# Folding the channels a second time per slot, with pooled queries as 128 and 16

## The chip, the cores and the metric

The kernel runs on one NeuronCore of a Trainium2 chip. Its engines are TensorE (PE, with its weight loads shown as PEld), VectorE (DVE), ScalarE (ACT), GpSimd (POOL) and SyncE (SP, which here only issues DMAs). The metric is the device time of one launch in microseconds, the median of several runs.

## The reference

Inputs q, k and v have the shape (8 batches, 8 heads, 576 positions, 64 channels); w_ch1 is 512 x 2048 and w_ch2 is 2048 x 512. All is float32.

```python
# attention: pooled by 4, and local within a band of |i - j| < 4
q_d, k_d, v_d = (x.reshape(B, H, 144, 4, D).mean(axis=3) for x in (q, k, v))
out_up = np.repeat(softmax_attention(q_d, k_d, v_d), 4, axis=2)
out_local = softmax_attention_masked(q, k, v, mask=abs(i - j) < 4)
x = heads_side_by_side(out_up + out_local)          # (8, 576, 512)
# mixing: the real part of a Fourier transform over positions and channels
mixed = np.real(np.fft.fft(np.fft.fft(x, axis=1), axis=2))
u = x + mixed
# feed-forward on the normalised rows
un = (u - mean(u)) / sqrt(var(u) + 1e-6)
out = u + relu(un @ w_ch1) @ w_ch2
```

## The kernel before

The work has two stages that overlap. In the first, for each of the 8 batches, attention and the Fourier mixing run; their results go to two tensors in HBM, `ud` (the pooled result, each row repeated four times) and `um` (the local result plus the mixed one). In the second, the feed-forward network (FFN) takes nine blocks of 512 rows, in four tiles of 128 each. A block's tile is loaded from `um` by SP and then `ud` is added to it by an accumulating DMA that POOL issues (`Block.load`, L695 to 707). Then come statistics and normalisation (L709 to 726), transposition on PE (L728), splitting into a high and a low part (L737 to 745), and the two products of the network (L754 to 781).

Matrix products here use a float32 type that PE takes rounded, so each operand is split: a high part by a rounding copy on ACT, and a low part by a subtraction, on POOL or DVE. A product is then three: high by high, high by low, low by high.

**Attention.** `Unit` (L352) is one of five local units per batch; each computes two windows of 64 positions for all 8 heads. `Pooled` (L240) works on two heads at a time: scores, maxima (DVE), exponentials (ACT), transposition of the probabilities (PE), a copy (ACT), the product with the values and the division (DVE). It has 144 queries in two halves of 72 (`GH`), and the results lie in `odt`, 72 partitions by 2 halves by 512 channels. The local results lie in `xa` (positions from the start) and `xb` (from the end), three slots of 128 partitions each; of the third slot only rows 0 to 63 are used and the rest is cleared once (L221).

**Mixing.** `Mix` (L506) uses symmetry. `half_sum` (DVE, L514) and `half_difference` (POOL, L518) fold the positions: x(s) + x(-s) and x(s) - x(-s). Then `channels_even` and `channels_odd` (DVE, L528 to 535) fold the channels: c with 512 - c, 256 channels each, for three local slots and for the two halves of `odt`. `split_high` (ACT) and `split_low` (POOL) make the operands `fh` and `fl`. `sequence` (PE, L564) transforms the positions: for each of 4 groups T of 128 channels, 3 x 5 products of 320 columns against the cosine and sine tables `seqm` and `seqg`. `sequence_z` (L580) does the same for the middle channel, which the folding leaves over. After another splitting, `mix` (PE, L593) transforms the channels: for each of three slots, an even and an odd part of 512 columns, 6 products each, and one more for the middle channel. `mixed` (DVE, L609) adds that to the local result, `unfold` (POOL, L615) undoes the folding of positions, and `store` (SP, L623) writes `um`.

**The order of the work** is written out by hand. Each piece is put on a timetable by `at(t, fn)`; all pieces are sorted by t and issued in that order, and each engine then runs its own queue strictly in order. `PACE` is 20, so batch b's pieces lie near t = 20 b; a step of the timetable is no fixed time. The numbers are in the table `AT` (L22 to 52). For batch b, `mix_at(b)` is 20 b plus the entry `mix`; from there, `halves` gives the first half sum, its step per slot, the first half difference and its step; `splits` the same for folds and splits; `z` and `sequence` the sequence products; `mixed` the first mix product, the step between the six of them, and the delays of `mixed`, `unfold` and `store`. The pooled part has its own start `pooled_at(b)` and end `pooled_end(b)`.

**Memory** is reused in four steps. At `t_b` the pooled part's tiles are given up (`close_b`, L830) and the four tiles of block 0 (`uts[0]`) take their place. At `t_a` the local part's are given up (`close_a`, L835), and there the tiles of block 1, the transposed operands `unT0`, more buffers for the weights and four PSUM banks for the FFN's results come in. `t_e` and `t_d` (L846, L852) follow when the tables of sequence and of channels are no longer needed. The weights arrive in an 8-byte form and are rebuilt by ACT, POOL and DVE in quarters of a tile pair (`Quarter`, L135); the first three tile pairs during attention, the next ones from `t_a` on.

**The passage from attention to FFN** goes so: block 0 is loaded from `t_b` on (L862), normalised from `t_a` on (L864), and its first five tile pairs of weights (`ROUND`) run, then five of block 1, while the last batch is still mixed.

## Time and profile before

| what | value |
|---|---|
| median of 3 runs | 1250.82 us (1249.33 to 1250.82) |
| the profiled execution, its time | 1254.06 us |
| its span, first to last instruction | 1252.0 us |
| mean granted PE clock | 0.967 of full speed |
| PE, PEld busy | 1184.1, 981.2 us |
| DVE, ACT, POOL busy | 590.7, 356.0, 318.2 us |
| read from and written to HBM | 81.82 MB, 28.34 MB |

A page of the profile gives the busy time of each engine as a union of its instructions' intervals, the span in 40 slices with the busy share in tenths, the chain of work that ended last, and groups of instructions by line. In a group's row, the line and the engine come first, then the operation, what it writes and reads, its shapes and count, then the busy time and the mean length of one, then the engine's idle time just before and who ended it. PE's matrix products are pipelined: the length of one is longer than the distance from one to the next, and what a series costs is read from the chain's pieces or the timeline. A row of a table of stretches gives each engine's busy time in that stretch, the granted clock, the share of the DMA engines and what they moved.

### The profile page before, as it was taken

How to read it: one execution, taken by the hardware profiler on the slowest of the kernel's cores; microseconds unless marked ns; L12 is line 12 of the kernel's file. 1: busy time of each engine (PE TensorE's matmuls, PEld its weight loads, DVE VectorE, ACT ScalarE, POOL GpSimd, SP SyncE). 2: the span in 40 equal slices, each digit the busy share in tenths (PEclk: the TensorE clock that was granted, in tenths of full speed). 3: DMA queues.
4: the chain of work that ended last, by engine and by line, in shares of the span. 5: the costliest groups of instructions: out<-in, count | busy, mean ns of one | idle time of the engine just before them, and what ended most of it. 6: DMA issues, size and time to landing. Idle time of an engine off the chain costs nothing.

```text
span 1252.0 us, 20525 instructions
## 1 busy us (share of the span) xinstructions
PE 1184.1 (95%) x8336; PEld 981.2 (78%) x8336; DVE 590.7 (47%) x1218; ACT 356.0 (28%) x1038; POOL 318.2 (25%) x397
## 2 busy tenths in 40 slices
PE   5889998899995699999999999999999999999998
PEld 5777887787984578888888888888888888888887
DVE  3767778698877788853222222122122222221211
ACT  3655454555562333431111111111011111111100
POOL 2226355365456566531010010000100100100000
PEclk7888998999997799999999999999999999999999
DMA  9755484565645525314040120210400400300000
GB/s 293 197 169 134 128 238 110 162 196 172 163 127 153 133 77 155 119 51 101 5 97 1 52 50 1 78 25 1 99 3 1 101 1 1 101 1 1 34 1 34
DMA packets 50462, 111.45 MB, mean 89 GB/s; under 512 B 6120, under 2 KB 6248, under 8 KB 50040
## 3 DMA queue, kind: packets, MB, share of 16 engines
q1 hardware_dynamic: 42000, 88.66, 22.6%
q0 software_dynamic: 8368, 21.48, 9.3%
q8 instruction: 66, 1.08, 0.4%
q14 instruction: 28, 0.23, 0.1%
HBM read 81.82 MB, written 28.34 MB: 88 GB/s over the span
## 4 chain that ended last, share of the span: by engine, by line
PE 81%; DVE 10%; DMA 6%; POOL 1%; SPq 1%; issue 1%; ACT 1%; POOLq 0%
PE hps L761 31%; PE acc L779 10%; PE acc L781 10%; PE acc L780 10%; PE y L569 4%; PE mix L607 4%; DMA vsum<-in_vg_dram 3%; PE av L452 2%; DMA qkT<-in_qk_dram 2%; PE avd L307 2%; PE sc L393 1%; DVE sums L379 1%; DVE xeo L535 1%; PE tpn L732 1%; PE sp L262 1%
## 5 line engine op out<-in xcount | busy, mean ns | idle before, releaser
L761 PE MATMUL hps<-unT,w1h 128*128 128x512 f32 x1152 | 311.5, 392 | 0.6 <-DVE yl L578 0.6
L769 DVE SCALAR_TENSOR_TENSOR hl<-hps,hh 128x512 fp32r<-128x512 f32 x144 | 99.3, 690 | 437.3 <-ACT hh L765 437.3
L761 PEld LDWEIGHTS hps<-unT,w1h 128*128 128x128 f32 x1152 | 215.2, 188 | 46.7 <-DVE yl L578 0.8
L765 ACT ACTIVATE hh<-hps 128x512 fp32r<-128x512 f32 x144 | 86.2, 598 | 512.1 <-PE hps L761 512.0
L779 PE MATMUL acc<-w2h,hh 128*128 128x512 f32 x576 | 226.5, 393 | 0.0
L781 PE MATMUL acc<-w2h,hl 128*128 128x512 f32 x576 | 225.1, 391 | 0.0
L780 PE MATMUL acc<-w2l,hh 128*128 128x512 f32 x576 | 225.0, 391 | 0.0
L761 PE MATMUL hps<-unT,w1l 128*128 128x512 f32 x576 | 155.2, 391 | 0.0
L761 PEld LDWEIGHTS hps<-unT,w1l 128*128 128x128 f32 x576 | 108.1, 188 | 23.8
L781 PEld LDWEIGHTS acc<-w2h,hl 128*128 128x128 f32 x576 | 108.2, 188 | 23.6
L779 PEld LDWEIGHTS acc<-w2h,hh 128*128 128x128 f32 x576 | 108.1, 188 | 22.9
L780 PEld LDWEIGHTS acc<-w2l,hh 128*128 128x128 f32 x576 | 108.2, 188 | 22.8
L717 POOL TENSOR_TENSOR rstd<-rstd,mhalf 128x1 f32<-128x1 f32 x36 | 20.3, 564 | 341.4 <-DVE rstd L716 341.4
L704 POOL DMA_DIRECT2D ut<-ud x40 | 35.5, 1111 | 208.0 <-DMA ut<-um 207.7
L607 PE MATMUL mix<-chanm,yh 128*128 128x512 f32 (+1 forms) x192 | 65.8, 425 | 5.6 <-DVE xs L611 3.7
L411 ACT ACTIVATE sb<-sc,mx 128x64 f32<-128x64 f32 x320 | 69.8, 329 | 1.3
L741 DVE TENSOR_TENSOR unT<-tpn,unT 128x512 fp32r<-128x512 f32 x36 | 24.8, 690 | 90.4 <-ACT unT L738 90.4
L547 POOL TENSOR_TENSOR fl<-xeo,fh 128x512 fp32r<-128x512 f32 (+1 forms) x40 | 56.0, 1404 | 30.5 <-ACT fh L542 30.2
L379 DVE TENSOR_REDUCE sums<-qkT 128x224 f32<-128x896 f32 (+4 forms) x48 | 44.5, 947 | 27.9 <-DMA qkT<-in_qk_dram 19.6
L520 POOL TENSOR_TENSOR xm<-xa,xb 128x512 f32<-128x512 f32 x24 | 34.2, 1427 | 87.9 <-DVE xb L470 79.9
L738 ACT CAST unT<-tpn 128x512 fp32r<-128x512 f32 x36 | 21.0, 586 | 113.5 <-PE tpn L732 113.5
L452 PE MATMUL av<-vaug,pT 64*64 64x65 f32 x1280 | 48.5, 227 | 1.7 <-DVE odt L322 1.5
(102 smaller groups left out, 1579.7 us busy)
## 6 DMA issues: line engine op xcount, KB each, us to landing
qkT<-in_qk_dram SPq DMA_DIRECT2D x40, 512.0 KB
raw<-in_wq_dram SPq DMA_DIRECT2D x64, 256.0 KB
vaug<-in_vw_dram SPq DMA_DIRECT2D x40, 260.0 KB
ud<-odt SPq DMA_DIRECT2D x16, 576.0 KB
out_dram<-ut SPq DMA_DIRECT2D x36, 256.0 KB
ut<-um SPq DMA_DIRECT2D x32, 256.0 KB
ut<-ud POOLq DMA_DIRECT2D x32, 256.0 KB, 5.6
vsum<-in_vg_dram POOLq DMA_DIRECT2D x24, 292.5 KB, 4.5
```

What stands on the lines that cost most here:

```text
L379: nc.vector.tensor_reduce(out=to, in_=x[:, :, a - g0 : e - g0], axis=AX.X, op=ALU.add)
L411: nc.scalar.activation(out=self.sb[:, a], in_=self.sc[:, a * W : (a + 1) * W], func=AF.Exp, scale=0.125, bias=self.mx[:, a : a + 1],)
L452: nc.tensor.matmul(av[r, a, :], pT[r, 4 * hh + a], va[r, 4 * hh + a, :], start=True, stop=True)
L547: nc.gpsimd.tensor_sub(out=l, in0=self.x[t], in1=h.bitcast(F32))
L569: nc.tensor.matmul(y, l, r, start=(i == 0), stop=(i == len(mms) - 1))
L607: nc.tensor.matmul(to, l, r, start=(i == 0), stop=(i == len(mms) - 1))
L761: nc.tensor.matmul(hps, a[:, c, :], unT[:, x, c, :], start=(i == 0), stop=(i == len(mms) - 1))
L765: nc.scalar.activation(out=hh, in_=self.hps[f], func=AF.Relu)
L769: nc.vector.scalar_tensor_tensor(out=hl, in0=self.hps[f], scalar=0.0, in1=self.hh[f].bitcast(F32), op0=ALU.max, op1=ALU.subtract)
L779: nc.tensor.matmul(acc, hh, w2h, start=start, stop=False)
L780: nc.tensor.matmul(acc, hh, w2l, start=False, stop=False)
L781: nc.tensor.matmul(acc, hl, w2h, start=False, stop=stop)
```

## The change

- **Channels folded a second time.** After the first fold, c with 512 - c (`channels`, on DVE, now both signs by one function and 255 channels wide), a second one folds c with 256 - c (`fold`): the sums on DVE, the differences on POOL, 2 x 128 channels each. Channels 0 and 256 go apart, with four columns in `z` in place of two. The groups T are now: sums and differences of the even fold, sums and differences of the odd fold. Even output channels need only two of the groups and odd ones the other two, so the channel table `chanm` has 256 columns in place of 512, and `mix` makes two half-width series where there was one of full width. `mixed` reads the two halves interleaved.
- **Pooled queries as 128 and 16.** In place of two halves of 72, the first 128 queries are one operand, and the last 16 go into rows 64 to 79 of the third local slot of `xa`, which were free. So the sequence products have four operands per series in place of five, and the table `seqg` is gone: its rows lie in `seqm`, which has a fourth slot. Maxima are four reductions per pair of heads in place of two, and the division has two multiplications in place of one. Storing the pooled result takes four DMAs in place of three.
- **Block 0's tokens loaded early.** `uts[0]` is a tile of its own from the start; its loads are on the timetable at 120, 124, 128 and 132, the accumulating ones 2.47 later. Block 0's normalisation is tied to `t_b` in place of `t_a`, and its operands lie in the memory given up at `t_b`.
- **Order set anew.** Nearly all entries of `AT` change.

```diff
-    "mix": (18.44, 18, 18),
+    "mix": (25.1, 24, 22.86, 21.7, 21.69),
-    "halves": (0.26, 3.82, 0.35, 3.58),
-    "splits": (1.11, 4, 0.49, 1.7, 2.25),
-    "z": (0.86, 9.92, 12.49, 12.91, 14.07),
-    "sequence": (13.12, 1.11, 2.15, 3.28),
-    "mixed": (19.5, 1.61, 1.13, 2.66, 2.85),
+    "halves": (0.3, 1.85, 0.35, 1.8),
+    "splits": (0.5, 1.8, 0.3, 0.6, 0.87, 1.4, 2),
+    "z": (0.14, 4.65, 7.44, 7.9, 8.9),
+    "sequence": (8.39, 1.11, 2.07, 3.07),
+    "mixed": (14.09, 1.4, 1.03, 2.53, 7.14),
-    "ffn": (7.51, 1.51),
+    "ffn": (4.81, 1.52),
-    "add": (2.5, 2.04, 2.98),
+    "add": (2.47, 0.77, 3.17),
...
+    queries = [(P, slice(0, P)), (G - P, slice(P, G))]
...
         def maxima(self, h0):
+            for t, (n, _) in enumerate(queries):
+                for hl, sp in enumerate(self.sps[h0]):
+                    i = 2 * t + hl
+                    nc.vector.tensor_reduce(
+                        out=mx[:n, i : i + 1], in_=sp[:n, t, :], axis=AX.X, op=ALU.max, negate=True
+                    )
...
         def result(self, h0):
+            for t, r in enumerate(rows):
+                to = (xa[r, NSL - 1] if t else odt)[:, h0 * D : (h0 + 2) * D]
+                nc.vector.tensor_mul(
...
+        def channels(self, t, odd):
+            if self.w.get(t) is None:
+                self.w[t] = psq.tile([P, 2, HD], F32, name="w", bufs=2)
+            src = odt if t == NSL else halves[self.b % 2][odd][:, t]
+            nc.vector.tensor_tensor(
+                out=self.w[t][:, odd, 1:HD],
+                in0=src[:, 1:HD],
+                in1=src[:, DM - 1 : HD : -1],
+                op=ALU.subtract if odd else ALU.add,
+            )
+        def fold(self, t, minus):
+            eng, op = (nc.gpsimd, ALU.subtract) if minus else (nc.vector, ALU.add)
+            w = self.w[t]
+            eng.tensor_tensor(
+                out=self.x[t][:, 2 * minus : 2 * minus + 2, :],
+                in0=w[:, :, 1 : P + 1],
+                in1=w[:, :, HD - 1 : P - 1 : -1],
+                op=op,
+            )
...
         def slots(self, x, odd, i):
-            groups = [(x[:GH, NSL + t], seqg[:, i, odd, t, :]) for t in range(2)]
-            return groups + [(x[:, t], seqm[:, i, odd, t, :]) for t in reversed(range(NSL))]
+            return [(x[:, t], seqm[:, i, odd, t, :]) for t in (NSL, NSL - 1, *range(NSL - 1))]
...
         def mix(self, t, odd):
+            for half, T in enumerate((3, 1) if odd else (0, 2)):
+                to = ps[:, half * HD : (half + 1) * HD]
+                for i, (l, r) in enumerate(((lh, mh), (lh, ml), (ll, mh))):
+                    nc.tensor.matmul(
+                        to, l, r, start=(bool(odd) and i == 0), stop=(i == 2), skip_group_check=True
+                    )
...
-            at(t_b + 0.1 + 0.1 * i + AT["add"][0] * pooled, blocks[0].load, i, pooled)
+            at(120 + AT["add"][0] * pooled + 4 * i, blocks[0].load, i, pooled)
...
-            (blocks[0], t_a, AT["first_norms"]),
+            (blocks[0], t_b, AT["first_norms"]),
```

More of the change, by code (lines that the diff above doesn't have):

```diff
@@ L77 @@
     c_signs: bass.AP,
-    c_group: bass.AP,
     out: bass.AP,
@@ L129 @@
     nc.vector.memset(mhalf, -0.5)
+    uts = {0: [res.tile([P, DM], F32, name=f"ut0{i}") for i in range(TILES)]}
+    unTs = {}
     ident = res.tile([P, P], F32, name="ident")
@@ L203 @@
     pd = p1.enter_context(tc.tile_pool(name="pd", bufs=1, side="right"))
-    odt = pd.tile([GH, 2, DM + 2], F32, name="odt")
-    nc.gpsimd.memset(odt[:, :, DM:], 0.0)
+    odt = pd.tile([P, DM + 2], F32, name="odt")
+    nc.gpsimd.memset(odt[:, DM:], 0.0)
+    rsd = pd.tile([P, 2, 2], F32, name="rsd")
+    nc.gpsimd.memset(rsd, 1.0)
     pbank = ExitStack()
@@ L286, in transpose_p @@
                 for kt in range(2):
-                    for t in range(2):
+                    for t, (n, cols) in enumerate(queries):
                         nc.tensor.transpose(
-                            tp[:, kt, t * GH : (t + 1) * GH],
-                            self.sd[h0][:, 2 * hl + t, kt * GH : (kt + 1) * GH],
-                            ident[:GH, :GH],
+                            tp[:, kt, cols],
+                            self.sd[h0][:n, 2 * t + hl, kt * GH : (kt + 1) * GH],
+                            ident[:n, :n],
                         )
@@ L302, in values @@
         def values(self, h0):
-            av = self.av[h0] = bank("avd", GH)[:, : 4 * (D + 1)].rearrange("p (t h d) -> p t h d", t=2, h=2)
+            av = self.av[h0] = bank("avd")[:, : 4 * (D + 1)].rearrange("p (t h d) -> p t h d", t=2, h=2)
             for hl in range(2):
-                for t in range(2):
+                for t, (n, cols) in enumerate(queries):
                     for kt in range(2):
                         nc.tensor.matmul(
-                            av[:, t, hl, :],
-                            self.pts[h0][hl][:, kt, t * GH : (t + 1) * GH],
+                            av[W * t : W * t + n, t, hl, :],
+                            self.pts[h0][hl][:, kt, cols],
                             self.vs[:, kt, h0 + hl, :],
@@ L500, in constants @@
         nc.gpsimd.dma_start(out=signs, in_=c_signs)
-        nc.gpsimd.dma_start(out=seqg, in_=c_group)
     def clear_yz():
@@ L539, in split_high @@
             if self.fh is None:
[L540 to L542 removed]
+                self.fh, self.fl = (psq.tile([P, NSL + 1, 4, P], F32R, name=f"f{part}", bufs=1) for part in "hl")
+            nc.scalar.copy(out=self.fh[:, t], in_=self.x[t])
         def split_low(self, t):
[L545 removed]
@@ L644, in plan @@
                 at(t + first_m + step_m * i, self.half_difference, slot)
-            for begin, name, these in (
-                (pooled_end(self.b), "pooled_splits", (NSL, NSL + 1)),
-                (t, "splits", local),
-            ):
-                first, step, odd, high, low = AT[name]
+            for begin, name, these in ((pooled_end(self.b), "pooled_splits", [NSL]), (t, "splits", local)):
+                first, step, odd, minus, plus, high, low = AT[name]
                 for i, slot in enumerate(these):
                     u = begin + first + step * i
-                    at(u, self.channels_even, slot)
-                    at(u + odd, self.channels_odd, slot)
+                    at(u, self.channels, slot, 0)
+                    at(u + odd, self.channels, slot, 1)
+                    at(u + minus, self.fold, slot, 1)
+                    at(u + plus, self.fold, slot, 0)
                     at(u + high, self.split_high, slot)
@@ L831, in close_b @@
         p1.close()
-        early = pool("early")
-        uts[0] = [early.tile([P, DM], F32, name=f"ut0{i}") for i in range(TILES)]
+        pools["early"] = pool("early")
+        unTs[0] = pools["early"].tile([P, 2, NCC, TILES * P], F32R, name="unT0")
     def close_a():
```

188 lines of the change are left out of this document (82 added, 106 removed).

## The prediction

> **What bounds the kernel now.** I read the page first, then a table with one row per batch, then the chain of waits, then the waits at the place where attention gives way to the feed-forward network (FFN).
>
> ```profile
> span 1252.0 us, 20525 instructions
> PE 1184.1 (95%) x8336; PEld 981.2 (78%) x8336; DVE 590.7 (47%) x1218; ACT 356.0 (28%) x1038; POOL 318.2 (25%) x397
> ```
>
> PE is busy for 95% of the span, so work taken from PE could be worth its length. But VectorE (DVE) at 47% is an average over two stages with different limits. The table of stretches, cut where each batch's sequence-z products start (columns: stretch, length, busy time of PE, PEld, DVE, ACT, POOL with counts, granted clock, DMA share, GB/s):
>
> ```profile
> 0.00:67.60 67.60, 47.05 (x716) 41.00 (x717) 39.66 (x94) 33.69 (x122) 20.34 (x35) 0.79 0.83 247
> 67.60:116.90 49.30, 46.14 (x588) 38.74 (x589) 36.15 (x83) 25.78 (x93) 19.61 (x19) 0.94 0.50 138
> 116.90:170.40 53.50, 49.08 (x604) 41.11 (x604) 39.68 (x92) 27.43 (x99) 26.44 (x29) 0.90 0.56 157
> 170.40:220.84 50.44, 46.85 (x590) 39.19 (x589) 39.43 (x88) 26.62 (x95) 22.47 (x24) 0.93 0.59 161
> 220.84:268.60 47.76, 42.82 (x544) 35.64 (x544) 37.04 (x81) 24.83 (x91) 24.78 (x27) 0.96 0.61 171
> 268.60:316.60 48.00, 45.77 (x642) 39.19 (x637) 42.28 (x97) 28.42 (x102) 26.81 (x29) 1.00 0.64 176
> 316.60:360.00 43.40, 43.26 (x589) 36.80 (x588) 38.51 (x87) 26.00 (x94) 23.81 (x25) 1.00 0.52 149
> 438.00:470.00 32.00, 31.70 (x143) 24.74 (x142) 27.98 (x49) 11.30 (x27) 19.41 (x26) 1.00 0.26 75
> ```
>
> Six periods run from 67.6 to 360.0: 48.73 us each on average, PE busy 45.65, DVE busy 38.85. PE is the fuller engine, at 0.937 of a period, but DVE is close behind (its best share is 38.51 of 43.40, 0.887). The last row shows PE full once the FFN runs. Between the two lies a hole:
>
> ```profile
> 392.00:408.00 16.00, 0.08 (x1) 0.00 (x0) 8.77 (x21) 1.84 (x5) 11.19 (x12) 0.57 0.89 229
> 408.00:424.00 16.00, 8.28 (x41) 5.78 (x41) 9.43 (x19) 3.91 (x9) 11.57 (x16) 0.71 0.72 164
> 424.00:431.00 7.00, 6.57 (x32) 6.53 (x33) 6.66 (x17) 2.90 (x9) 2.93 (x5) 0.69 0.65 172
> ```
>
> PE idles 15.9 + 7.7 + 0.4 = 24.1 us, and what it does there at clocks of 0.71 and 0.69 loses 8.28 x 0.29 + 6.57 x 0.31 = 4.4 us more. The waits of that place (from 370 to 445 us; engine and line, whom it waited for, total, times, longest) and two pieces of the chain say why:
>
> ```profile
> PE tpn L732 <- DVE un L724: 18.6, 3, 16.3
> DVE st L713 <- DMA ut<-ud: 7.0, 1, 7.0
> PE y L569 <- DVE unT L741: 5.4, 1, 5.4
> 396.82 8.17 DMA ut<-ud
> 417.11 5.30 DMA raw<-in_wq_dram
> ```
>
> Block 0's tokens are loaded only when attention closes. DVE waits 7.0 us for them with the last batch's folding queued behind that wait, and PE waits for both. A second stop of 5.4 us comes from weights that arrive late.
>
> **What PE loses.** Three pieces of the chain at full clock, and the group of weight loads:
>
> ```profile
> 360.23 1.46 PE yz L585 x10
> 361.69 2.24 PE y L569 x15
> 379.07 3.02 PE mix L607 x13
> L569 PEld LDWEIGHTS y<-seqm,fh 128*128 128x128 f32 x192 | 33.3, 202 | 0.0
> ```
>
> A sequence product takes 2.24 / 15 = 0.149 us for 320 columns. Four pooled rows of operands per chain become one, so each of the 4 chains of a batch has 12 products, not 15: 12 x 0.149 = 1.8. The z chain has 8 instead of 10: 2 x 0.146 = 0.3. A mix product takes 3.02 / 13 = 0.232 for 512 columns; 36 of the 39 per batch shrink to 256 columns. From 0.149 and 0.232 the slope is 0.083 / 192 columns, so 256 columns come to 0.121; the bound above is 0.149, the row with more columns. I take 0.126, near the slope: 36 x 0.106 = 3.8. Together 5.9 us per batch, 47 over eight. Four products of scores, four transpositions and eight value products per pair of heads keep their number and columns (128 + 16 for 72 + 72): nothing.
>
> **What DVE gains.** Rows of the batch from 316.6 to 360.0 (group, shapes, count, busy us, mean ns of one, idle before):
>
> ```profile
> L267 DVE TENSOR_REDUCE mxd<-sp 72x2 f32<-72x288 f32 x8 | 3.2, 444 | 0.0
> L406 DVE TENSOR_REDUCE mx<-sc 128x8 f32<-128x512 f32 x5 | 3.4, 682 | 0.0
> L318 DVE TENSOR_SCALAR rsd<-avd 72x4 f32<-72x4 f32 x4 | 0.6, 150 | 0.3 <-PE avd L307 0.3
> L322 DVE TENSOR_TENSOR odt<-avd,rsd 72x256 f32<-72x256 f32 x4 | 1.7, 420 | 0.1
> L531 DVE TENSOR_TENSOR xeo<-xs 128x256 f32<-128x256 f32 x3 | 2.8, 922 | 0.0
> L531 DVE TENSOR_TENSOR xeo<-odt 72x256 f32<-72x256 f32 x2 | 1.6, 790 | 0.0
> L535 DVE TENSOR_TENSOR xeo<-xm 128x256 f32<-128x256 f32 x3 | 1.3, 418 | 0.0
> L535 DVE TENSOR_TENSOR xeo<-odt 72x256 f32<-72x256 f32 x2 | 0.9, 474 | 0.0
> ```
>
> Maxima: the two reductions differ by 238 ns over 224 elements, 1.06 ns each. Eight of 288 elements become sixteen of 144, each 0.29 us alone and, by the overlap of the row (8 x 444 ns in 3.2 us), 0.25 in a row: 4.0, so +0.8. Results: per pair of heads one more 0.15 and two multiplications of 128 elements (420 - 136 = 284 ns) for one of 420: +0.3, times four, less overlap, +1.0. Folding: ten operations in 6.6 us become twelve of the same size (eight first folds, four sums; the four differences go to POOL): 12 x 0.66 = 7.9, +1.3. If all ran at the 0.41 of the undisturbed ones, it would be 4.9, so -1.7. Sum +3.1 (from 0 to +6): DVE goes from 38.85 to 42.0 per batch while PE goes to 39.8. DVE becomes the fuller engine.
>
> Why the same operation takes 0.42 or 0.92 shows in three lines of the timeline:
>
> ```profile
> 337.51 0.68 DVE L516 TENSOR_TENSOR xs<-xa,xb 128x512 f32<-128x512 f32 x1
> 345.04 1.27 POOL L520 TENSOR_TENSOR xm<-xa,xb 128x512 f32<-128x512 f32 x1
> 345.13 1.74 DVE L516 TENSOR_TENSOR xs<-xa,xb 128x512 f32<-128x512 f32 x1
> ```
>
> The sum takes 0.68 us alone and 1.74 when POOL's difference is running: it ends 0.56 after POOL does. If every new difference on POOL holds up DVE in this way for its whole length, the change can lose; that is the slower rival below, at 1269 us. The Trainium skill (SBUF — State Buffer, SBUF: two separate sides) has it as a rule: a VectorE operation with two SBUF inputs and a GpSimd operation that reads SBUF take an exclusive lock on a shared pair of ports, and the second waits until the first has ended. By that rule, the trace agrees: 1.74 is about what is left of POOL's operation and a whole sum.
>
> **The period.** At 0.937 full, 42.0 gives 44.8 us; at DVE's own best share of 0.887 it gives 47.3. I take 45.2, nearer the first: in steps of the timetable (20 to a batch; worked out from its rows mix, halves, splits and mixed) the old one lays half sums and folds at 18.3 to 29.4 over the mixing of the batch before at 17.5 to 26.7; the new one lays mixing at 15.8 to 23.8 and folds at 22.0 to 27.8, so fewer operations of DVE and POOL should meet. That is 3.5 us times six periods, 21 us.
>
> **The last two batches.** Batch 7's sequence and mix products lie where PE is full beside FFN work, so 5.9 counts whole. Batch 6's lie just ahead of the hole, where DVE finishes last: I count half, 3.
>
> **The hole.** Loading block 0 early moves four loads on SP and four accumulating ones on POOL into the seventh batch's time:
>
> ```profile
> L704 POOL DMA_DIRECT2D ut<-ud x40 | 35.5, 1111 | 208.0 <-DMA ut<-um 207.7
> ```
>
> The issue costs POOL 4 x 1.1 us, beside 24 of 43 busy: hidden. POOL's load waits for SP's to land, and differences and low parts queue behind it; the two are 2.47 steps apart, 6.0 us at 48.73 / 20 per step, against at most the 8.17 of the chain's piece: up to 2.2 us per load, which POOL's idle time holds. Batch 6's store stood behind two of the late weight fetches in SP's order and now stands behind four, which removes most of the 5.4. What remains is the last batch's own chain:
>
> ```profile
> 396.20 1.23 DVE L516 TENSOR_TENSOR xs<-xa,xb 128x512 f32<-128x512 f32 x1
> L542 ACT CAST fh<-xeo 128x512 fp32r<-128x512 f32 x3 | 1.9, 618 | 1.9 <-DVE xeo L535 1.9
> L547 POOL TENSOR_TENSOR fl<-xeo,fh 128x512 fp32r<-128x512 f32 x3 | 3.8, 1275 | 3.0 <-ACT fh L542 3.0
> L190 POOL TENSOR_TENSOR w1l<-wt,w1h 128x256 fp32r<-128x256 f32 x2 | 1.4, 724 | 2.5 <-ACT w1h L186 2.5
> ```
>
> PE stopped at 392.1, and DVE came to the last half sum at 396.2 without the load's wait. From there: sum 1.23, two first folds 0.84, POOL's difference 0.72 (a POOL operation of 256 elements, the last row), high part 0.62, low part 1.28, and some 0.5 of hand-overs, 5.2 us: the first product at 401.4, 9.3 us of idle. Normalising block 0 falls into the same stretch on DVE; at most the 8.8 us that DVE was busy from 392 to 408, of which I take 3, because PE transposes that block meanwhile. So 12 of idle and 1.5 of slow clock against 28.5: 15 us gained, bounds 5 and 25.
>
> **Waits that come new.** A slot's high part on ACT now waits for POOL's difference too; behind it stand the exponentials of the next unit. At most 4 x 0.72 = 2.9 us per batch, on an engine that is busy 26 of 43: nothing, but it may delay the scores' banks. The 16 pooled queries lie in the local slot, so DVE's next pooled result waits until the half sum, the half difference and the store have read them: 3.8 and 4.6 steps, 9 to 11 us, nothing. One more store per batch on SP, and four short scalings more on ACT: nothing.
>
> The clock is a further cost of an idle PE:
>
> ```profile
> 114.00:120.00 6.00, 3.05 (x19) 1.55 (x20) 4.24 (x14) 3.65 (x12) 2.29 (x3) 0.81 0.72 182
> 120.00:126.00 6.00, 6.00 (x33) 5.58 (x31) 2.38 (x7) 2.34 (x10) 3.73 (x6) 0.50 0.75 184
> ```
>
> After a stretch half idle PE runs 6 us at half clock, so 3 us are lost after 3 us of waiting. In the six periods the granted clocks of 0.94, 0.90, 0.93, 0.96, 1.00 and 1.00 cost 12.7 us of PE's busy time. A PE that waits for DVE may pay this more often, but then it has time to spare; I leave it inside the 45.2 and the range.
>
> **Sum.** 21 + 3 + 5.9 + 15 = 44.9. The profiled execution took 1254.06 us (span 1252.0): 1209.2. It lies 3.2 above the median of 1250.82, so 1206. Batch 0 is left as it is: its tables shrink by 1.1 MB (4.5 us of DMA at the 247 GB/s of the first row), worth 0 to 4.
>
> **Rivals.**
> - *PE's saving counts whole.* Periods shrink by 5.9: 6 x 5.9 + 5.9 + 5.9 + 20 = 67, time 1184. For it: the period from 316.6 with PE never idle. Against: 42.0 of DVE would need a 42.8 period at 0.98.
> - *DVE eats the saving.* At 47.3 per period, 6 x 1.4 + 5.9 + 10 = 24, time 1227. For it: DVE was never above 0.887.
> - *The half-width products cost nearly as much as before.* A weight load lasts 202 ns; if that set the pace, mix saves 36 x 0.030 = 1.1 instead of 3.8. Batch 7 loses 2.7 and the periods about 1 each: 1215. Against: 0.149 for a sequence product, which has the same load and is shorter than 202.
> - *Slower: the lock.* The four POOL differences of 256 elements (0.72 us) each hold DVE for their whole length, +2.9, so DVE needs 44.9, and keeps its 9.9 us of idle per period since what it waits for stays: 54.8. That is +6.1 x 6 + 3 less 15 and 5.9, time 1269. It decides from a period of about 51.7: then six periods and batch 6 cost the 20.9 that the hole and batch 7 bring. By the skill's page on SBUF this is what the lock can do at worst; the batch from 316.6, with 0.42 beside 0.92 for one kind of fold, shows that it strikes about half the time, hence the small chance.
>
> **How the numbers follow.** Forecast 0.47, whole saving 0.22, eaten 0.16, half-width 0.06, slower 0.09. The forecast's own range is 1195 to 1218. From 1178 to 1232 takes in the first four with their bounds and leaves out the slower case and the tails. A measurement can tell about 0.2%, 2.5 us. Faster 0.88 (the first four less a tail), same 0.03, slower 0.09.
>
> **What would show it.** Mix products of 256 columns 0.12 to 0.15 apart; y chains of 12 in about 1.8 us; periods near 45 with DVE at 0.9 or more and PE below it; more DVE folds longer than 0.8 us if the lock rules; PE's idle between the last local products and the first FFN products near 12 us instead of 24, with no DVE wait for block 0's load. The prediction is wrong if periods stay at 48 or above, if PE's idle there stays over 20, or if the periods fall below 43.

## The result, and the profile after

The change makes the kernel slower: 1295.06 us (1293.29 to 1296.65, 4 runs) against 1250.07 us (1248.92 to 1250.82, 4 runs) of the kernel before on the same chip, a ratio of 1.036 (95% interval 1.0342 to 1.0378), 45 us where a gain of 45 was forecast. The page of the changed kernel:

```profile
span 1292.6 us, 20563 instructions
PE 1216.6 (94%) x8224; PEld 993.8 (77%) x8224; DVE 637.3 (49%) x1362; ACT 360.3 (28%) x1062; POOL 336.0 (26%) x421
```

PE has 112 products fewer and is busy 32.5 us longer. DVE has 46.6 us more to do, POOL 17.8. The same table as before the prediction, cut where each batch's sequence-z products start (stretch, length, busy time of PE, PEld, DVE, ACT, POOL with counts, granted clock, DMA share, GB/s):

```profile
81.47:130.21 48.74, 45.93 (x526) 37.14 (x524) 38.62 (x91) 25.02 (x90) 21.55 (x24) 0.92 0.49 134
130.21:186.08 55.87, 50.82 (x575) 41.14 (x574) 46.59 (x111) 28.71 (x105) 27.65 (x32) 0.85 0.51 144
186.08:239.86 53.78, 45.78 (x556) 37.62 (x554) 43.86 (x100) 24.42 (x89) 25.27 (x28) 0.87 0.51 139
239.86:293.52 53.66, 50.68 (x575) 40.74 (x573) 43.35 (x102) 26.82 (x97) 27.60 (x30) 0.85 0.58 162
293.52:351.06 57.54, 53.56 (x575) 43.00 (x573) 45.89 (x107) 27.36 (x98) 28.14 (x30) 0.80 0.57 160
351.06:405.03 53.97, 48.05 (x575) 38.47 (x574) 45.01 (x107) 27.22 (x98) 29.18 (x33) 0.91 0.54 135
405.03:462.58 57.55, 39.56 (x397) 32.99 (x396) 41.60 (x102) 20.85 (x68) 25.13 (x30) 0.77 0.30 90
462.58:1292.60 830.02, 820.62 (x3681) 674.68 (x3679) 282.70 (x521) 143.22 (x287) 127.06 (x183) 1.00 0.18 49
```

The account of the 40.6 us between the two spans: the first batch's mixing starts at 81.5 instead of 67.6 (+13.9); seven periods take 381.1 us instead of 344.4 (+36.7); what follows the last batch's z products takes 830.0 instead of 840.0 (-9.9). The six periods compared in the prediction average 53.9 us, not 45.2 and not the old 48.7. DVE is busy 43.9 of them, or 0.81, and PE 49.1, or 0.91, at clocks of 0.80 to 0.92: neither is full over a period. Something inside the period holds both.

One period in slices shows where (same columns, from 270 us on):

```profile
270.00:276.00 6.00, 6.00 (x69) 4.33 (x67) 5.66 (x12) 1.43 (x4) 3.94 (x7) 1.00 0.82 193
276.00:282.00 6.00, 3.88 (x74) 3.46 (x74) 5.97 (x12) 3.38 (x14) 3.91 (x5) 0.86 0.84 253
282.00:288.00 6.00, 6.00 (x31) 3.63 (x28) 5.72 (x12) 2.69 (x7) 5.24 (x5) 0.50 0.88 292
288.00:293.50 5.50, 4.64 (x68) 3.99 (x68) 4.07 (x8) 2.07 (x10) 5.42 (x5) 0.50 0.40 110
```

From 270 to 288 us DVE is nearly full (5.66 to 5.97 of 6). PE idles 2.1 us, then its clock falls to 0.50, and in 282 to 288 it gets through 31 products, after 69 and 74 (in part of other kinds) in the two slices before. The timeline of that stretch (start, length, engine, line, what is written and read; in brackets the engine's idle time before it and who ended it):

```profile
276.44 1.75 DVE L526 TENSOR_TENSOR xs<-xa,xb 128x512 f32<-128x512 f32 x1
278.22 0.42 DVE L538 TENSOR_TENSOR w<-xs 128x255 f32<-128x255 f32 x1
...
279.29 0.40 PE L397 MATMUL sc<-maskb,identb 64*64 64x512 bf16 x2 [2.12 <-DVE xs L633]
...
281.82 1.71 POOL L530 TENSOR_TENSOR xm<-xa,xb 128x512 f32<-128x512 f32 x1
282.50 1.30 DVE L538 TENSOR_TENSOR w<-xs 128x255 f32<-128x255 f32 x1
283.49 1.45 POOL L565 TENSOR_TENSOR fl<-xeo,fh 128x512 fp32r<-128x512 f32 x1
283.73 1.49 DVE L551 TENSOR_TENSOR xeo<-w 128x256 f32<-128x256 f32 x1
```

DVE's lines are half sums and folds of the local slots. In the lines left out it also has maxima and `mixed` between them, and just ahead, from 273.3 to 276.4, it rebuilds weights. PE waits 2.12 us until DVE has done a `mixed` (L633) that stands in this queue. The same fold lasts 0.42 us at 278.22, where POOL does nothing, and 1.30 at 282.50, beside POOL's half difference, ending 0.27 after it. The Trainium skill (SBUF — State Buffer, SBUF: two separate sides) says that of a VectorE operation with two SBUF inputs and a GpSimd operation that reads SBUF, the one that starts first blocks the other for its whole length; the trace agrees, with the end of the fold 0.27 us behind the end of POOL's operation.

### The profile page after: what moved, and what is told of

It is laid out like the page before. It is cut to its first block, busy times and chain, and to the rows that moved or that the text cites. A ratio compares the mean times of both kernels' runs of the same rounds, so it can differ in the third digit from the quotient of the medians.

```text
span 1292.6 us, 20563 instructions
## 1 busy us (share of the span) xinstructions
PE 1216.6 (94%) x8224; PEld 993.8 (77%) x8224; DVE 637.3 (49%) x1362; ACT 360.3 (28%) x1062; POOL 336.0 (26%) x421
## 4 chain that ended last, share of the span: by engine, by line
PE 76%; DVE 13%; POOL 4%; DMA 2%; issue 2%; ACT 2%; SPq 0%; POOLq 0%; DVEq 0%
PE hps L779 30%; PE acc L799 10%; PE acc L797 10%; PE acc L798 10%; PE y L587 4%; PE avd L312 3%; DVE w L538 2%; DMA vsum<-in_vg_dram 2%; PE tp L293 2%; PE av L463 2%; PE sc L404 1%; DVE xs L526 1%; DVE xeo L551 1%; DVE wt L173 1%; PE mix L626 1%
## 5 line engine op out<-in xcount | busy, mean ns | idle before, releaser
L779 PEld LDWEIGHTS hps<-unT,w1l 128*128 128x128 f32 x576 | 108.1, 188 | 23.8
L312 PE MATMUL avd<-vsum,ptd 72*128 72x65 f32 (+1 forms) x512 | 65.2, 268 | 2.4 <-DMA vsum<-in_vg_dram 1.5
L759 DVE TENSOR_TENSOR unT<-tpn,unT 128x512 fp32r<-128x512 f32 x36 | 24.7, 689 | 84.3 <-ACT unT L756 84.3
L293 PE MATMUL tp<-ident,sd 128*72 128x128 f32 (+1 forms) x256 | 53.9, 270 | 11.5 <-DVE xm L633 6.4
L312 PEld LDWEIGHTS avd<-vsum,ptd 72*128 72x128 f32 (+1 forms) x512 | 53.4, 156 | 12.2 <-DMA vsum<-in_vg_dram 1.7
L463 PE MATMUL av<-vaug,pT 64*64 64x65 f32 x1280 | 54.1, 243 | 8.9 <-issue 7.0
L293 PEld LDWEIGHTS tp<-ident,sd 128*72 128x72 f32 (+1 forms) x256 | 29.6, 116 | 40.2 <-issue 17.4
L463 PEld LDWEIGHTS av<-vaug,pT 64*64 64x64 f32 x1280 | 48.2, 155 | 14.5 <-issue 8.9
```

The lines of the kernel that those rows point to most:

```text
L293: nc.tensor.transpose(tp[:, kt, cols], self.sd[h0][:n, 2 * t + hl, kt * GH : (kt + 1) * GH], ident[:n, :n],)
L312: nc.tensor.matmul(av[W * t : W * t + n, t, hl, :], self.pts[h0][hl][:, kt, cols], self.vs[:, kt, h0 + hl, :], start=(kt == 0), stop=(kt = ...
L463: nc.tensor.matmul(av[r, a, :], pT[r, 4 * hh + a], va[r, 4 * hh + a, :], start=True, stop=True)
L779: nc.tensor.matmul(hps, a[:, c, :], unT[:, x, c, :], start=(i == 0), stop=(i == len(mms) - 1))
```

## The experiments

The kernel before took 1251.67 to 1254.66 us beside these runs; each ratio is to the runs beside it, and differences of medians to the changed kernel are good to some 4 us (an estimate from the spread of the kernel before, 1250.07 to 1254.66). Three theories stood at first: that it costs when PE changes between widths (M), that a load of 128 columns costs more than one of 72 (W), and that DVE's extra work sets the period (D). Later came a fourth, that the new timetable costs (O).

**Wide products first.** In transpositions and value products the loop over 128 and 16 becomes the outer one; nothing else changes.

```diff
...
-            for hl in range(2):
-                for t, (n, cols) in enumerate(queries):
+            for t, (n, cols) in enumerate(queries):
+                for hl in range(2):
```

> The changed kernel, with the products of the 128-query operand first and those of the 16-query operand behind them, in the transpositions and in the value products (same work, other order inside each step). Theory M (every change between a 128-wide and a 16-wide operand stops PE for about 0.1 us): per pair of heads 12 of the 18 changes go, transpositions fall from 1.48 to about 0.85 us and value products from 1.74 to about 1.15, 1.2 us per pair, 38 us over the kernel where PE sets the pace: time 1255 to 1270. Rival W (an operand of 128 columns takes longer to load than one of 72): both stay at 1.48 and 1.74, time 1295. Rival D (DVE, 5 us more per batch, sets the pace): the pieces shrink as in M, the time stays at 1285 to 1295.

1280.42 us, ratio 1.0232 (1.0196 to 1.0267): 14.6 us of the 45, between what M (1255 to 1270) and what D and W (1285 to 1295) had foretold. Eight transpositions and sixteen value products of a pair of heads, each with what comes behind them, in the kernel before, the changed one and this one, from their timelines:

```profile
328.87 1.19 PE L307 MATMUL avd<-vsum,ptd 72*72 72x65 f32 x16
329.87 0.54 PE L569 MATMUL y<-seqg,fh 72*128 72x320 f32 x2
...
364.51 0.69 PE L288 MATMUL tp<-ident,sd 72*72 72x72 f32 x8
365.13 1.15 PE L452 MATMUL av<-vaug,pT 64*64 64x65 f32 x32
```
```profile
306.78 1.55 PE L293 MATMUL tp<-ident,sd 128*72 128x128 f32 x8
308.26 1.15 PE L463 MATMUL av<-vaug,pT 64*64 64x65 f32 x32
...
314.55 1.81 PE L312 MATMUL avd<-vsum,ptd 72*128 72x65 f32 x16
316.28 0.48 PE L619 MATMUL mix<-signs,yz 128*128 128x512 f32 x1
```
```profile
255.74 0.88 PE L292 MATMUL tp<-ident,sd 128*72 128x128 f32 x8
256.55 0.51 PE L624 MATMUL mix<-chanm,yh 128*128 128x256 f32 x2
...
258.77 1.56 PE L310 MATMUL avd<-vsum,ptd 72*128 72x65 f32 x16
260.26 1.15 PE L461 MATMUL av<-vaug,pT 64*64 64x65 f32 x32
```

The distance from the series to its successor is what it costs: 0.62 us before, 1.48 after, 0.81 with the widths grouped. Six changes of width fewer save 0.67 us, 0.11 each (M, for the transpositions). The Trainium skill says that a change of the tiling mode drains PE (TensorEngine Tiling (Array Packing), Key Properties), without a price; a cost per change would fit that, but no run here shows whether 16 rows beside 128 are such a change. The value products fall only from 1.73 to 1.49, where sixteen with 72 columns had taken 1.00 here and 1.09 in the median of the attention stage. What stays when the widths are grouped is what W foretold; that it comes from the loads is not shown.

**Early load undone.** Block 0's tiles, loads and normalisation put back as in the kernel before.

```diff
...
-            at(120 + AT["add"][0] * pooled + 4 * i, blocks[0].load, i, pooled)
+            at(t_b + 0.1 + 0.1 * i + AT["add"][0] * pooled, blocks[0].load, i, pooled)
...
```

> The changed kernel, with block 0 loaded and normalised as before, at the end of attention. All theories: the hole returns; from the traces (last sequence-z to the end: 840 us before, 830 after) about 10 us more, 1300 to 1310. If the early load's waits on POOL and SP are what slows the periods, it is faster instead: below 1280.

1301.69 us, ratio 1.041 (1.0372 to 1.0448). The early load gains, but some 6.6 us and not the 15 forecast for the hole.

**Second folding with the new order, and with the old.** Both kernels have the second folding but two halves of 72 queries and no early load. The first keeps the new timetable, the second has the old one. With the new order:

```diff
...
-    queries = [(P, slice(0, P)), (G - P, slice(P, G))]
...
+    seqg = psq.tile([GH, 2, 2, 2, NK1], F32R, name="seqg")
...
```

> The changed kernel without the pooled queries as 128 and 16 (two halves of 72 as before) and without the early load; the second folding and the new order stay. Theory M: no changes of width, PE per batch falls below that of before (mix 4 us less), so time 1230 to 1255. Rival D, if it is the folding that loads DVE: still slow, 1270 to 1300.

With the old one (here the folds of a slot follow at 0.8 and 1.1 behind its first):

```diff
...
-    "halves": (0.3, 1.85, 0.35, 1.8),
+    "halves": (0.26, 3.82, 0.35, 3.58),
...
```

> The kernel before with the second folding alone, in the old order (two halves of 72, late load). Theory M: PE 4 us less per batch, 1225 to 1250. Rival D (folding): DVE 2 to 3 us more per batch and POOL's differences in its way, 1255 to 1280. Beside the run without the split of queries but in the new order this tells what the new order is worth.

1307.03 us, ratio 1.0443 (1.0413 to 1.0474), and 1265.55 us, 1.0119 (1.0076 to 1.0161). The folding alone loses 13 us, although PE is busy 14.0 us less (1170.1): DVE has 27 us more. The new order adds 41 us to that; part of it may be that the first kernel also packs the folds of the two pooled halves into 0.7 steps (entry `pooled_splits`), closer than either timetable has them. Both ran without the change of widths, so M, which had foretold 1230 to 1255 for the first, is not the main cause. This was the turn: the order, which the prediction had counted as a gain, is the largest loss.

**The old order in the changed kernel.** Three kernels: the whole old timetable; the same with the wide products first; and the old entries for the mixing alone. In all three the half sum of the third slot runs ahead of the last pooled results that go into its free rows, so the mixing takes older rows there; number and size of the operations are those of the changed kernel.

```diff
...
-    "mix": (25.1, 24, 22.86, 21.7, 21.69),
...
-    "halves": (0.3, 1.85, 0.35, 1.8),
-    "splits": (0.5, 1.8, 0.3, 0.6, 0.87, 1.4, 2),
...
+    "mix": (18.44, 18, 18),
...
+    "halves": (0.26, 3.82, 0.35, 3.58),
+    "splits": (1.11, 4, 0.49, 0.8, 1.1, 1.7, 2.25),
...
```

> All parts of the change (second folding, 128 and 16 queries in free rows, early load), but every entry of the timetable as before (the three folds of a slot stand at +0.8, +1.1 and later in the old spacing of 4 per slot). Theory O (the new timetable, which lays the half sums and folds of three slots 1.8 apart in one stretch and the mixing after it, costs about 40 us, as the second folding with the new and with the old order show, 1307 against 1266): 1252 to 1265 us, periods of 50 to 52 us, first yz product near 71 us rather than 81. Rival D (DVE with 44 us per batch and the contention of the folds with POOL sets the period, whatever the order): 1285 to 1300 us, periods stay at 53 to 57.

> The old timetable as in the run before it, and the 128-wide transpositions and value products of a pair issued ahead of the 16-wide ones. If the two costs add (order 40 us, changes of width 15 us): 1238 to 1250 us, at or a little below the kernel before. If the period is set by DVE once the order is gone: within 5 us of the run before it.

> The changed kernel with only the timetable of the mixing as before (mix start, half sums, folds and splits, z, sequence products, mixed), while the start of the pooled attention, its steps, the loads of q, k and v and the early load keep the new one. Theory O, with its loss in the bunched folds: 1252 to 1270 us, close to the run with the whole old timetable. If the loss sits in the shift of pooled attention and loads against one another: 1285 to 1300 us.

1272.21 us (1.011 to 1.021), 1265.37 (1.0069 to 1.0133) and 1267.2 (1.0085 to 1.0168). The third is where O put it; the first lies between O and D, and the second, 7 us below the first, fits neither of its two expectations. So the entries of the mixing carry most of it, and D alone does not: all seven periods average 49.5 to 50.0 us, for 54.4 in the changed kernel and 49.2 in the kernel before, with the same 1362 operations on DVE. The 96 folds among them take 59 to 61 us in place of 75.2. But 13 to 20 us over the kernel before remain, and these kernels do not wait for the free rows. And the reason for the new order shows. The last pooled result of a batch lands 24.9 steps after 20 b in batch 0 and 20.9 in the last ones (`pooled_at` + 15 + 9.41), while the old timetable sums the third slot, where 16 of those rows now lie, at 18.3 to 18.7. The free rows forbid that.

**The folding's differences on DVE.** The prediction's slower rival named these 32 POOL operations as what holds DVE up.

```diff
-            eng, op = (nc.gpsimd, ALU.subtract) if minus else (nc.vector, ALU.add)
+            eng, op = nc.vector, ALU.subtract if minus else ALU.add
```

> The changed kernel with the differences of the second folding on DVE in place of POOL (32 operations more on DVE, none of this kind on POOL). By the lock rival of the prediction (each difference on POOL holds DVE for its own length) DVE gets the work but loses the waits: the mean of the folding operations w and xeo falls from 0.75 to 1.0 us towards 0.5 us, DVE's busy time rises by no more than 10 us and the time is 1270 to 1297 us. Without contention: the means stay, DVE's busy time rises by some 24 us (32 by 0.75), and the time rises to 1300 to 1325 us.

1295.26 us, ratio 1.0338 (1.0297 to 1.0378), no different from the changed kernel. DVE's busy time rises by 13.0 us and POOL's falls by 27.6, and on balance neither is felt. DVE's folds become 128 and take 97.7 us, 0.76 each, after 75.2 us for 96, or 0.78: they do not get shorter. So these differences are not what stretches the folds.

**Third slot second.** An order that the free rows allow: slot 1, then slot 2, then slot 0, 1.9 steps apart, the mixing started nearly as early as before, wide products first.

```diff
...
-            local = list(reversed(range(NSL)))
+            local = [1, 2, 0]
...
```

> All parts of the change and the wide products first, with an order that is the old one except that the slot with the free rows is summed second instead of first (slot 1 at step 4, slot 2 at 5.9, slot 0 at 7.8 after the start of mixing, which is 19.5, 18.6 and 18 steps), so that the 16 pooled rows are in it in time. In the runs with the old order the half sums of this slot came ahead of the last pooled results. Theory O in its narrower form (the free rows forbid the early half sums, and it is the bunching of sums and folds behind the pooled attention that costs): the three slots lie 1.9 steps apart here too, so little is won on the changed kernel with the wide products first: 1268 to 1280 us, periods 51 to 54 us. If it was the late start of the mixing (25.1 and 21.7 steps) that cost: 1245 to 1265 us, as with the old order.

1292.99 us, ratio 1.0331 (1.0296 to 1.0366): outside both expectations, and worse than the narrow form of O allowed. It is also 12.6 us above the wide products first with the new order. The early start of the mixing brought nothing here, with the three slots as close as before; why it lost, no run shows.

**Useless products in PE's idle time.** Since PE's clock falls after its idle time in the stretch, this fills it.

```diff
+            for _ in range({4: 18, 0: 8}.get(self.m, 0) if self.u >= 4 else 0):
+                to = self.av[0].rearrange("p h d -> p (h d)")
+                nc.tensor.matmul(to, seqm[:, 0, 0, 0, :P], seqm[:, 0, 0, 0, : 4 * (D + 1)], start=True, stop=True)
```

> The changed kernel with useless products put on TensorE ahead of the value products of two of a batch's five local units (18 and 8 products of 260 columns, into a bank that the value products overwrite), where TensorE waits for DVE in the stretch of the folds: about 3 us of work more per batch. Theory C (TensorE's idle time in that stretch costs twice, because the granted clock stands at 0.50 for the 12 us behind it): the clock stays nearer 1.00, the periods fall by 1 to 5 us and the time to 1260 to 1290 us, though TensorE has more to do. If the stretch of DVE and POOL alone sets the period: 1293 to 1300 us. If TensorE's own work is the path: up to 1318 us.

1292.84 us, ratio 1.0324 (1.0283 to 1.0365), and these two slices in place of the second and third above:

```profile
276.00:282.00 6.00, 5.98 (x98) 4.94 (x98) 5.86 (x12) 3.39 (x14) 3.99 (x5) 1.00 0.93 274
282.00:288.00 6.00, 3.59 (x20) 2.60 (x20) 5.79 (x12) 2.72 (x9) 5.24 (x5) 0.83 0.57 223
```

The clock is back, PE does more, and the time does not move: the seven periods take 3.3 us less together, and the first batch starts 3.2 later. PE finishes sooner and then waits for DVE, 2.41 us ahead of the transpositions at 285.56. So the half clock is here a sign of the stall more than what costs.

**Slots spread again.** Same order as the third-slot-second kernel, 3.3 to 3.5 steps apart.

```diff
...
-    "halves": (4, 1.9, 4.1, 1.8),
-    "splits": (4.2, 1.9, 0.3, 0.6, 0.87, 1.4, 1.9),
+    "halves": (4, 3.3, 4.1, 3.3),
+    "splits": (4.3, 3.5, 0.49, 0.8, 1.1, 1.7, 2.2),
...
```

> All parts of the change, wide products first, and the three slots' half sums and folds spread again (slot 1 at step 4, slot 2 at 7.3, slot 0 at 10.6 after the start of mixing at 18.44 and 18 steps; spacing 3.3 to 3.5 where the change has 1.8 and the kernel before about 4), with the slot of the free rows in second place, so that the pooled rows are in it in time; the products follow 0.7 steps later than in the old timetable. Theory O (bunching: DVE full, folds stretched by POOL's subtractions beside them, TensorE waiting): periods of 48 to 51 us, 1250 to 1268 us. If it is the slot of the free rows itself, or the folding's DVE work wherever it lies: 1278 to 1295 us.

1307.85 us, ratio 1.0454 (1.0412 to 1.0495), a miss for O's number. The waits from 67 to 420 us (engine and line, whom it waited for, total, times, longest) say why:

```profile
DVE xa L479 <- POOL xm L528: 35.1, 7, 7.0
```

Now slot 0's half difference stands at 28.7 steps, and the next batch's first local result, which overwrites slot 0, at 29.3. POOL is late, and DVE waits for it seven times. So this order has no room behind. By the timetable slot 2 has to go between the pooled results (20.9 to 24.9) and the next batch's first one (25.9 in the last batches), and slot 0 between 25.3 and 29.3; slot 1 has until 33.3. By these numbers slot 1 could go last, with the three slots spread. No run tried that, so it is not shown that the free rows force a close order.

**The new timetable in the kernel before.** Nothing but the entries of the mixing.

```diff
...
-    "halves": (0.26, 3.82, 0.35, 3.58),
-    "splits": (1.11, 4, 0.49, 1.7, 2.25),
...
+    "halves": (0.3, 1.85, 0.35, 1.8),
+    "splits": (0.5, 1.8, 0.3, 1, 1.6),
...
```

> The kernel before, unchanged but for its timetable of the mixing, which takes the changed kernel's (start at 25.1 to 21.7 steps, half sums 1.85 apart, folds 1.8 apart, products from step 8.4 on). No second folding, no 128 and 16, no early load. Theory O: the timetable alone costs most of what the change lost: 1275 to 1295 us. If the bunching hurts only together with the second folding's DVE and POOL work: 1248 to 1262 us.

1296.0 us, ratio 1.0347 (1.0316 to 1.0378). The timetable alone makes the old kernel as slow as the whole change does. Of the cost, 12.8 us are the first batch's later start and 31.6 the seven periods, where the whole change has 13.9 and 36.7. That the two totals agree is partly chance: the change has other costs besides (the widths) and a gain (the early load).

**The third slot moved, in the kernel before.** `local = [1, 2, 0]` with slots 1.9 steps apart; start, products and everything else as before. The half sums of slots 1 and 0 stay within 0.1 of their places; their folds come 0.9 to 1.1 steps earlier and their splits 1.5 to 1.7, so that not quite one thing alone moves.

```diff
-    "halves": (0.26, 3.82, 0.35, 3.58),
-    "splits": (1.11, 4, 0.49, 1.7, 2.25),
+    "halves": (4, 1.9, 4.1, 1.8),
+    "splits": (4.2, 1.9, 0.49, 1.1, 1.7),
...
```

> The kernel before with one thing moved: the half sums, folds and splits of slot 2 (the slot that has the free rows) stand second, 1.9 steps behind slot 1's, instead of first, 4 steps ahead of them; start of the mixing, products and all else stay. Theory O (bunching of the three slots' sums and folds behind one another): most of the loss, 1275 to 1295 us. If the later start of the mixing, the pooled attention or the products' steps cost: 1250 to 1262 us.

1289.02 us, ratio 1.0286 (1.0245 to 1.0326): 34 us, with one slot's half sums moved by 5.6 steps and the folds packed. The folds of that kernel and of the kernel before, to 500 us (count, busy us, mean ns, idle before):

```profile
L531 DVE TENSOR_TENSOR xeo<-xs 128x256 f32<-128x256 f32 x24 | 22.8, 948 | 7.8 <-POOL fl L547 6.8
L535 DVE TENSOR_TENSOR xeo<-xm 128x256 f32<-128x256 f32 x24 | 21.6, 901 | 0.0
```
```profile
L535 DVE TENSOR_TENSOR xeo<-xm 128x256 f32<-128x256 f32 x24 | 17.1, 714 | 0.0
L531 DVE TENSOR_TENSOR xeo<-xs 128x256 f32<-128x256 f32 x24 | 13.0, 541 | 1.2 <-POOL fl L547 1.2
```

The same 48 operations take 44.4 us instead of 30.1, as they would if they now meet POOL's differences and low parts, and DVE waits 6.8 us for POOL's low parts, 1.2 before. That is 20 of the 34 us at most. For the rest there is only an argument so far: DVE's queue is long where PE waits for its end. PE's wait for DVE's pooled results (`av` for `odt`, 67 to 420 us) goes from 1.5 to 8.2 us. The next run bears on it.

**Weight decoding moved out of the stretch.** In the changed kernel, 5 steps earlier.

```diff
-    "decode": (49.7, 10.23, 5.84, 1.23, 2.62),
+    "decode": (44.7, 10.23, 5.84, 1.23, 2.62),
```

> The changed kernel with the decoding of the weights (3.2 us on DVE twice in a period) begun 5 steps earlier, so that it no longer drifts into the stretch of the half sums and folds (it stands at 273, 331 and 389 us in the profile of the changed kernel, just before and inside that stretch). If DVE's queue in that stretch is the path: the later periods fall by up to 3 us each, 1278 to 1290 us. If DVE's queue there is not the path: 1292 to 1300 us.

1279.82 us, ratio 1.0212 (1.0173 to 1.025): some 15 us less than the change, for moving the same work. The decoding has parts on ACT and POOL too (in the stretch above, POOL's low part of the weights runs for 1.52 us just ahead of the half difference at 281.82), and they move with it. So the queues of that stretch are on the path; that it is DVE's alone is not shown.

**Half differences on DVE**, in the changed kernel and in the kernel before.

```diff
-            nc.gpsimd.tensor_sub(out=xm[:, t, :DM], in0=xa[:, t], in1=xb[:, t])
+            nc.vector.tensor_sub(out=xm[:, t, :DM], in0=xa[:, t], in1=xb[:, t])
```

> The changed kernel with the half differences (three per batch, 1.3 to 1.7 us each on POOL) on DVE in place of POOL. If POOL's operations stretch DVE's beside them (fold operations 0.42 us alone, 1.3 to 1.5 us beside a POOL subtraction): DVE gets three operations of some 0.7 to 1.1 us more per batch, but its folds fall from means of 1.00 and 0.81 us to about 0.5, and the time falls to 1270 to 1288 us. If only the sum of DVE's work in the stretch counts: 1305 to 1320 us.

> The kernel before with the half differences on DVE in place of POOL. Its sums and folds are spread over 8 steps, so there is less to win: 1240 to 1255 us if the contention costs here too (a version that beats both), 1258 to 1275 us if DVE's added work counts.

1284.09 us, ratio 1.0264 (1.0216 to 1.0311), 11 us less than the change; and 1251.77 us, 0.9995 (0.9973 to 1.0017), no difference. The second folding's groups on DVE, to 500 us, in the changed kernel and with the half differences on DVE:

```profile
L538 DVE TENSOR_TENSOR w<-xs 128x255 f32<-128x255 f32 x24 | 23.9, 995 | 1.2
L551 DVE TENSOR_TENSOR xeo<-w 128x256 f32<-128x256 f32 x32 | 23.8, 751 | 1.4
L538 DVE TENSOR_TENSOR w<-xm 128x255 f32<-128x255 f32 x24 | 19.4, 808 | 7.0 <-POOL xm L530 7.0
L538 DVE TENSOR_TENSOR w<-odt 128x255 f32<-128x255 f32 x16 | 8.1, 514 | 0.1
```
```profile
L530 DVE TENSOR_TENSOR xm<-xa,xb 128x512 f32<-128x512 f32 x24 | 25.1, 1045 | 0.1
L551 DVE TENSOR_TENSOR xeo<-w 128x256 f32<-128x256 f32 x32 | 17.7, 557 | 5.4 <-POOL fl L565 4.2
L538 DVE TENSOR_TENSOR w<-xs 128x255 f32<-128x255 f32 x24 | 16.5, 688 | 0.2
L538 DVE TENSOR_TENSOR w<-xm 128x255 f32<-128x255 f32 x24 | 10.9, 454 | 0.1
L538 DVE TENSOR_TENSOR w<-odt 128x255 f32<-128x255 f32 x16 | 6.6, 418 | 0.1
```

DVE is given 25.1 us of work, and its folds fall from 75.2 to 51.7 us: the work is as good as free. POOL's half differences do hold DVE, in a bunched order; spread out, in the kernel before, moving them changes nothing on balance. Whether the 11 us come from the shorter folds or from POOL's shorter queue, the run does not tell.

**The early load in the kernel before.** Three of block 0's four tiles early; room for them comes from one buffer less for q and k and one less for v.

```diff
-NUM_V, NUM_QKT, NUM_P = 3, 6, 2
+NUM_V, NUM_QKT, NUM_P = 2, 5, 2
...
```

> The kernel before with three of the first block's four token tiles loaded early and normalised where the first of the two pools closes, as in the change; room for it comes from one buffer less of v (2) and one less of q and k (5), since the mixing matrices are not halved here. Early load worth 6.6 us as on the changed kernel, and the buffers not missed: 1244 to 1248 us, a version that beats both. If the fewer buffers cost more than that: 1253 to 1275 us.

1274.22 us, ratio 1.017 (1.0124 to 1.0216). A wait of this kernel, 67 to 420 us, against 11.6 us in the same row of the kernel before:

```profile
DVE sums L381 <- DMA qkT<-in_qk_dram: 37.4, 13, 6.2
```

PE in its turn waits 19.1 us for these sums, 2.5 before. Without the room that the free rows and the halved channel table make, the early load takes buffers that are needed.

**All three reliefs.** Wide products first, decoding earlier, half differences on DVE.

> The changed kernel with all three reliefs: the 128-wide transpositions and value products ahead of the 16-wide ones, the decoding of the weights begun 5 steps earlier, the half differences on DVE. If they are three costs: 1295 less 15, 15 and 11, 1248 to 1258 us, level with the kernel before. If they are one cost, the stretch in which DVE is full: 1268 to 1282 us.

1264.1 us, ratio 1.0106 (1.0068 to 1.0144). Together 31 us, where the three alone were worth 15, 15 and 11. That lies between the two expectations: the costs overlap in part. The first batch starts 10.3 us later than in the kernel before, the seven periods take 11.7 more, and what follows takes 11.4 less. It is the fastest kernel with all parts of the change, and still 1% slower than the kernel before. No version was found that beats both.

## Why the prediction was wrong

**The step that failed is the period's timetable.** The prediction read from `AT` that the new order lays folds (22.0 to 27.8) behind the mixing of the batch before (15.8 to 23.8) and concluded that "fewer operations of DVE and POOL should meet", taking 45.2 us. It compared folds with mixing and not folds with folds: the half sums and folds of three slots went from 11 steps to under 6. There DVE is full, its operations meet POOL's own half differences and low parts, and PE waits. The period was 53.9 us, and this timetable alone, in the kernel before, costs 43 us (1296.0 against 1253.35). The shares by which the prediction turned 42.0 us of DVE into a period (PE's 0.937 and DVE's best of 0.887) came from periods of the old order and said nothing of a new one: DVE's share in the new one is 0.81.

**Batch 0** was "left as it is", worth 0 to 4 us. But the entry `mix` puts its mixing at 25.1 steps in place of 18.44, and its z products came 13.9 us later.

**It also missed what forces the order.** It asked when DVE's next pooled result may write the free rows (9 to 11 us of slack, "nothing") and not the other direction: the third slot's half sum must now wait for the last pooled result, 2.6 to 6.2 steps later than it ran before. The early load in turn needs the room that the free rows and the smaller table make. So the parts of the change hang together, and the gain of 6.6 us was bought with a later third slot, and in this timetable with the close order.

**"Nothing" for the products that "keep their number and columns" was wrong.** (The prediction's numbers, four, four and eight, are those of one head; a pair has twice as many.) At full clock, a pair of heads costs 0.86 us more in transpositions (1.48 for 0.62) and 0.73 more in value products (1.73 for 1.00; 0.65 by the medians), some 6 us per batch, as much as the predicted saving of 5.9. Grouping the widths gave back 14.6 us of time. PE's other terms were right. Mix products, six of them at full clock:

```profile
434.04 0.40 PE L626 MATMUL mix<-chanm,yh 128*128 128x256 f32 x2
434.28 0.28 PE L626 MATMUL mix<-chanm,yl 128*128 128x256 f32 x1
434.39 0.40 PE L626 MATMUL mix<-chanm,yh 128*128 128x256 f32 x2
434.63 0.28 PE L626 MATMUL mix<-chanm,yl 128*128 128x256 f32 x1
434.75 1.81 PE L312 MATMUL avd<-vsum,ptd 72*128 72x65 f32 x16
```

From 434.04 to 434.75 they take 0.118 us each, where 0.126 was taken; a sequence series of 12 took 1.85 us, where 1.8 was taken.

**DVE's work:** +3.1 us per batch with a bound of +6 was predicted, +5.0 came. Folding is the term that was mis-sized: 75.2 us in 96 operations, 0.78 each, for the 0.66 that was taken. That makes 1.5 us of the 1.9 per batch.

**The hole:** 15 us were predicted (5 to 25). The changed kernel there:

```profile
440.00:456.00 16.00, 3.14 (x44) 2.39 (x43) 15.13 (x29) 2.27 (x5) 12.34 (x14) 0.63 0.54 158
456.00:472.00 16.00, 10.73 (x46) 7.98 (x47) 11.64 (x21) 4.83 (x11) 14.98 (x18) 0.62 0.51 130
472.00:480.00 8.00, 6.63 (x43) 6.13 (x42) 6.84 (x15) 2.64 (x8) 4.40 (x8) 1.00 0.85 187
```

PE idles 12.9 + 5.3 + 1.4 = 19.5 us, and 5.2 are lost to the clock: 24.7 against 28.5 before and 13.5 predicted. Where DVE waited for the load, it is now full (15.13 of 16): it normalises block 0, folds the last batch and rebuilds weights at the same place, and PE still waits 14.9 us for the normalised tiles (18.6 before). The 3 us taken for that was too little. The half counted for batch 6 and the whole for batch 7 (3 and 5.9) cannot be read apart from this; all that follows the last z products gained 9.9 us.

**The slower rival** had the right side and nearly the right period (54.8), but the wrong operation, so the nearness is luck. Its own POOL differences could move to DVE with no effect on balance. The lock that it named strikes through the old half differences and low parts, which the new order brings together with the folds; taking the half differences from POOL was worth some 11 us of the 45. What remains open is how the rest splits between DVE's bare queue and the waits of ACT and POOL in that stretch; no run separated these.

## What to carry to other kernels

Free memory is not free in time: rows shared between two producers make whoever reads them wait for the later one, so ask of every shared tile which reader now waits for which writer, and where its work then goes. Cost a timetable by the density of its fullest stretch on each engine, not by the mean of a period; and a new order can be tried alone, on the old kernel, before anything else is built. Products of different width on TensorE are best issued in runs of one width: here that gave 14.6 us.

## What the hardware showed that was not expected

- Eight transpositions that alternate between 128 and 16 rows cost 1.48 us, grouped by width 0.81, and eight of 72 rows 0.62: about 0.11 us for each change of width, an estimate from the first two.
- Sixteen value products, half with 128 and half with 16 stationary columns, cost 1.49 us even when grouped; with 72 columns 1.00 to 1.09. Both have the same sum of columns.
- Moving 24 subtractions of 512 elements from POOL to DVE lowered DVE's busy time from 637.3 to 631.8 us.
- Filling PE's idle time brought the granted clock of the six periods from 0.80 to 0.92 up to 0.88 to 1.00 and changed the time by nothing.
